# A fused attention and feed-forward kernel: another seven-product scheme in the first dense layer, chained in one PSUM bank, with a new written-out order

## The chip, the cores and the metric

One core of one Trainium2 chip. The metric is the device time of one execution in microseconds. TensorE (PE) multiplies matrices; VectorE (DVE), ScalarE (ACT) and GpSimd (POOL) work on tiles; SyncE (SP) and the POOL queue issue most transfers. Each engine works through its own instructions in the order in which the program gives them. The operands of the matrix products are bf16, the sums in PSUM fp32.

## The reference

```python
# q, k, v: (4, 8, 768, 64); n_sink 4, window 128; w_in: 512 x 2048; w_out: 2048 x 512
scores = q @ k^T / sqrt(64)                            # per batch and head, 768 x 768
keep = (key < 4) | ((query - key >= 0) & (query - key < 128))
a = softmax(where(keep, scores, -1e9))
x = (a @ v).transpose(0, 2, 1, 3).reshape(3072, 512)   # heads side by side
g = maximum(x @ w_in, 0) ** 2                          # 3072 x 2048
out = g @ w_out                                        # 3072 x 512
```

## The kernel before, in words

*How the program is put together.* The kernel first records some 945 operations (each a small function that emits one or a few instructions) and then emits them in the sequence of a written-out list of numbers, `ORDER` (L21 to L58). The suffix of a number names the engine where there is a choice (d is DVE, a is ACT, g is POOL), `+0` or `+1` the PSUM pool that a tile comes from. The tile framework adds the waits on data and on rooms; the order on each engine's queue is that of the list. `DUMMIES` (L59) gives some PE operations filler matmuls ahead of their own. Rooms are counted in L146: two PSUM tiles of two banks each in the pool att and two in den, which scores, values, products and outputs share, and in SBUF among others expm=8, qs=6, r=3.

*Batch by batch.* There are four batches of 768 rows, handled in steps of 256 rows (s = 0, 1, 2). For the attention of a step the score matmuls (L613) write PSUM, ACT takes the exponential into an `expm` room (L634), POOL (L218) or DVE masks it, the value matmuls (L682) follow, DVE normalizes (L698/L699) and the rows are turned into `xT`. Batch 0 at the very start has the longest way: q and k are loaded by SP in fp32 (qr, L351), cast to bf16 (L192, L194 or L195, the three engines' branches of one copy helper) and turned by PE (L507) for each of four pairs of heads, then copied out of PSUM. At the start POOL also makes the identity and the masks, the head rows (`build_head_rows`) and the scaled sink values (L554), and issues the loads of v, w_in and w_out. Batches 2 and 3 load q and k as rows and are turned by transposing transfers on SP (L461), and their attention outputs too (L713). The order spreads the attention of batch b+1 between the dense products of batch b.

*First dense layer.* Batch 0 has the plain form, `layer1` (L752, matmuls L763). Batches 1 to 3 have `layer1_fast` (L821), a seven-product (Strassen) form. The weights are cut into A00, A01, A10, A11 (first index: half of the 2048 features, second: half of the 512 inputs), the transposed rows into B00 to B11 (second index: half of the rows), and with sums of blocks made beforehand

```
m1 = (A00+A11)(B00+B11)   m2 = (A10+A11)B00      m3 = A00(B01-B11)   m4 = A11(B10-B00)
m5 = (A00+A01)B11         m6 = (A10-A00)(B00+B01)  m7 = (A01-A11)(B10+B11)
C00 = m1+m4-m5+m7   C01 = m3+m5   C10 = m2+m4   C11 = m1-m2+m3+m6
```

Weight sums come from `weight_sums_in` (L792, ten DVE operations once), row sums from `total` inside `layer1_fast` (three single and one double operation for each group of rows). `FAST` (L1281) names the row groups: in batch 1 steps (0, 1) as 512 rows and then step 2 as 256, in batches 2 and 3 step 0 as 256 rows and then (1, 2) as 512. Each group is worked through in quads (`quad`, L867): 18 quads, 12 with 28 matmuls over 256 columns and 6 with 56 over 128. A quad has one PSUM tile of two banks, 512 fp32 columns each. m1 goes to bank 0, m2 to bank 1; ACT or DVE copies bank 0 to an SBUF tile t (k1), DVE subtracts m2 (k2) and, when m5 has replaced m1 in bank 0, m5 (k3, both L936). m4 is added onto bank 1 and m3 onto bank 0; k4 rectifies both banks in one instruction of 1024 columns (L951 on ACT), a square follows (L917 on ACT, L919 on DVE), m6 and m7 are added on, and k5 (L963, a custom DVE operation: sum, bounded below by 0) adds t to both banks; a second square follows. All products of a quad are at L894.

*Second dense layer.* `layer2` (L969) for two steps of batch 0, `layer2_chain` (L1188, matmuls L1233) for nearly all others, `layer2_fast` (L1029) for the last. Outputs are copied to `osb` rooms and stored by SP.

Of the kernel before, what the change touches and what calls it, by code (L numbers as in the profile page):

```python
# [21 lines left out]
944 0 1 2 7 8 9 10 11 12 13 14 15 16 17 18 945+0 3 5 19 20 21 6 79 22 23 24 25 55d 56d 57+0 58 59d 60a 83+0 85 103+1  # L22
105 26 27 28 62d 61d 63+1 64 67d 68d 65a 69+0 70 71d 72d 66a 84+1 73a 74a 75+1 76 78d 91+0 86 77a 93 80 113+1 87+0
92+1 89 94 95+0 97 115 88 90 96 98 114+1 99+0 101 117 100d 104+0 81+1 102d 107 82 4 29 106g 30 31 32 33 34 35 36 37 38
39 40 41 42 43 44 45 46 127 47 48 49 50 116d 118d 108d 156+0 109+1 119+1 121 111 162+0 110 120 122 112 123+1 125 124d
126d 157a 163a 158a 164a 168+1 165+0 51 52 53 54 177+0 169a 170d 208g 166a 167a 178d 171+1 179a 172a 128+1 131+0 174+0
173a 132a 129d 319 323 321 175d 324 176d 322 130a 320 159+1 133a 160a 161a 278+0 279 136+1 144+0 145+0 280 281 148 138
146 289+1 149d 139d 274 147d 275 282 290 283 291 292 284 276 277 134+1 137+0 135 286a 140 141d 285 287d 293 150+0 151
294 142+1 196+0 192+1 295 143 193 200+1 198a 202a 195d 197 199d 201 203d 297d 194d 296 298a 152+1 154 204+0 205
212+0+1 153a 155d 189+0 215 206a 213 190a 214 207d 186+0 216 191d 248+0 187d 249d 251+1 209 253a 188d 252a 180+1 181d  # L30
250d 182d 183+0 326 184a 185d 300 301 230+0+1 233 299 288 219+0+1 231 220 304+0 210+0 306a 211 222 305 237+0+0 240
232d 325 302 221 303 223 241d 238 239d 311 307 217+1 254+0 224+0 308a 255 309 218 242+0 225 243 452g 422 423 424 425
426 427 428 429 430 431 432 433 434 234g 235+1 226+0 228 310a 227a 229a 314 236 244+0 246 316a 247a 327 313 245d 329
256+0+1 257 315 328 332 317 330 347+1 333+1 348 334 259 335a 337 312 336 331 338 349a 263+1+1 266 264 339 351 340 341a
350 352 435 436 437 258g 438 439 267g 265g 361+0 353 362 354 363d 260g 364 343 365 366 445 440 453 444 441 355a 356a
342a 448 446 449 442 447 443 451 450 318 344 345 357 375+0 358 376 261+0 359 377a 346a 367 368 379 378 262 380 268+0
270+0 381 382 360a 369a 271a 269 370d 371 272 273d 372 383a 389 373 463+0+0 385 386 466 464 390 408+0 409 394+1 395
410a 391 393 387 411 396a 397 412 456+1+0 413 392 414 398 400 415 374d 388a 457 384a 399 504 458 506 465 467 505 508+0
416a 401 418 419 510a 511 402a 654 655 684g 656 657 658 659 660 661 662 663 664 665 672 459 420 460 685 512a 417a 421a
403a 404 468+0 509 405 513 454+1 469 406 507 514a 455 515 461+0 472+1+0 407a 517 523 542 462 518 519 521 544 675 673  # L40
470 473 546+0 475 543 548a 479+0+0 516 520d 549 480 482 550a 524 481d 545 476d 525 483d 547 495+1+0 551 553 496 552a
498 556 674 676 666 667 668 474g 669 670 499g 471 522 679 488+0+0 555 554 526 497d 484+1 557 491 489 671 492g 490g
477+0 500+0 485 478 559 501 561 527+0 528 529d 563 562 493+0 565 558d 494 534 530 535 531d 566+0 567 532 533a 568d 569
564 570 572 571 536 683 682 677 678 486 502 680 711+0+0 487 503 573 574d 537 538 539d 540 681 541 560 714 712 704+0+0
580+0 581 576 577 582d 583 594 584 585 575a 705 707 688+0+0 713g 715g 706g 708g 689 691 578 586 587 626+1 627 588a
628a 612+0 686+0 613 687 630 596 692 690 595 629 631 716+0 717 589a 614a 632 633 579a 634a 635a 615 590 616 597 617
693+0 694 591 618 636 619 637 592 598+1 599 620a 600a 638 593a 601 622 640+0 641 602 623 642a 736 643 603 644 604 646
605 645 709+0 647 624 740+0 639a 621a 606a 648a 742a 649a 607a 608 609 738 737 650 651 743 739 710 610 611d 741
695+0+0 744a 625a 696 698 652 653d 755 697 699 756 757 745 747 746a 749 748 720+0+0 723 759+0 750 700+0 701 761a 762
751 721 752a 763a 760 722g 753 724g 727+0+1 774 775 758 728 730 725+0 766 764 778+1 779 765a 729d 767 776 726 777 768  # L50
731g 732+1 733 718 719 702 703 754 734 735 793 794 785 770 769 798+1 812+0 799 813 780a 771a 800a 814a 781 782a 797
796 786 772 795 815 801 802 816 817 818 803 783 819 784d 787 820a 804 805 789 822 823 829 826 827 828 791 806a 807a
821a 808 809 788 830+0 831 790a 832a 824 825d 810 858+1 811a 834 872+0 844+1 860a 846a 874a 833 835 836 837 873 845
859 876 838a 839a 886 887 888 875 877 861 840 841 848 862 864 792 773 842 863 847 889 849 878 879 890+0 865 843a 880a
850 882 883 851 892a 881a 866d 867d 884 893 894d 868 869 852a 853a 854 855 870 856 895 891 897 896a 885a 900 857d 871d
905 909+1 899 907 901 924 926 906 898 925 903 911a 912 913a 902a 928+1 904 914 910 929 931+1 915d 908 927 918 920 919
930a 933a 916 922 921d 934 917 923 932 935 936 939 937 938 943 940 942 941
"""  # L58
DUMMIES = {  # L59
    945: 29, 58: 8, 63: 10, 64: 4, 83: 3, 91: 3, 97: 3,  # L60
# [56 lines left out]
def kernel(  # L117
# [674 lines left out]
    def weight_sums_in(key, last):  # L792
# [4 lines left out]
        def room(e):  # L797
            if not tiles:
# [4 lines left out]
        spec = ((1, A[0][0], A[1][1], ALU.add, (0, 0), (0, 1)), (6, A[1][0], A[0][0], ALU.subtract, (0, 2), (1, 0)),  # L803
                (7, A[0][1], A[1][1], ALU.subtract, (1, 1), (1, 2)))
        for n, (name, x, y, how, *places) in enumerate(spec):
            for a, (d, j) in enumerate(places):
                def run(e, name=name, x=x, y=y, how=how, a=a, d=d, j=j):
                    room(e)
                    wi_sb[name, a] = tiles[d][:, j]
                    nc.vector.tensor_tensor(out=tiles[d][:, j], in0=x[:, :, a], in1=y[:, :, a], op=how)  # L810
                ops["wi", name, a] = op(key + 0.004 * (2 * n + a), {"dve": 0.7}, run, after=[w_in_op[i] for i in range(4)],
                                        takes=slots if n + a == 0 else [],
                                        follow=[ops["wi", 1, 0]] if n + a else [])
        for name, x, y, old in ((2, A[1][0], A[1][1], 6), (5, A[0][1], A[0][0], 7)):
            for a in range(2):
                def run(e, name=name, x=x, y=y, a=a):
                    wi_sb[name, a] = x[:, :, a]
                    nc.vector.tensor_tensor(out=x[:, :, a], in0=x[:, :, a], in1=y[:, :, a], op=ALU.add)
                ops["wi", name, a] = op(key + 0.03 + 0.004 * a, {"dve": 0.7}, run, after=[ops["wi", old, a]] + last)

    def layer1_fast(b, ss, key, step):  # L821
# [13 lines left out]
        whole = Slot("expm", 3 + 2 * nq)  # L835
# [9 lines left out]
        def total(names, x, y, how, n):  # L845
            pool = "qs" if len(names) * hw <= 256 else "expm"
            slot = Slot(pool, nq * len(names))
            P.group = ("xs", b, ss[0])

            def run(e):  # L850
                t = bank(slot, "xs", [128, 2 * len(names), hw], BF16)
                (nc.vector if e == "dve" else nc.gpsimd).tensor_tensor(out=t, in0=x(), in1=y(), op=how)  # L852
                for i, name in enumerate(names):
                    xs[name] = t[:, 2 * i:2 * i + 2]
            o = op(key(0) - 0.002 * (5 - n), {"dve": 0.18 + 0.26 * len(names) * hw / 256}, run,
                   after=landed, takes=[slot], reads=[whole] if len(ss) == 1 else [])
            for name in names:
                sums[name], slots[name] = o, slot
# [8 lines left out]
    def quad(b, ss, qd, key, xs, sums, slots, part, landed, whole):  # L867
# [4 lines left out]
        bs, ts, r1s, r2s = Slot(("den", "att"), 1), Slot("expm", 3), Slot("r", 1), Slot("r", 1)  # L872
# [3 lines left out]
        def weights(name, f, a):  # L876
            if name == 3:
                return w_in_sb[:, f // 4, a, f % 4:512:4]
            if name == 4:
                return w_in_sb[:, 2 + f // 4, 2 + a, f % 4:512:4]  # L880
            return wi_sb[name, a][:, f // 4, f % 4:512:4]
# [519 lines left out]
```

## Time and profile before

| what | value |
|---|---|
| time, median of 3 runs | 209.46 us (209.41 to 210.68) |
| span of the profiled execution | 208.3 us |
| granted clock of TensorE | 1.000 |
| busy: PE / DVE / ACT / POOL | 200.5 / 173.1 / 135.9 / 96.4 us |
| matmuls / DVE / ACT / POOL instructions | 2476 / 318 / 189 / 138 |
| moved by DMA | 26.10 MB |

The span goes from the first to the last instruction of one profiled execution; the time of a run holds some more, before and after. The page gives busy time by engine, the span in forty slices with the busy tenths of each, the chain of work that ended last (followed back from the end), and groups of instructions by source line. A row of a group reads: line, engine, operation, output and input with partitions x elements and type, count, then busy us and mean ns of one, then the idle time of that engine just before these instructions and what ended it. A busy PE is not PE at its peak, and the ends of matmuls are modelled.

### The profile page before, as it was taken

How to read it: one execution, taken by the hardware profiler on the slowest of the kernel's cores; microseconds unless marked ns; L12 is line 12 of the kernel's file. 1: busy time of each engine (PE TensorE's matmuls, PEld its weight loads, DVE VectorE, ACT ScalarE, POOL GpSimd, SP SyncE). 2: the span in 40 equal slices, each digit the busy share in tenths (PEclk: the TensorE clock that was granted, in tenths of full speed). 3: DMA queues.
4: the chain of work that ended last, by engine and by line, in shares of the span. 5: the costliest groups of instructions: out<-in, count | busy, mean ns of one | idle time of the engine just before them, and what ended most of it. 6: DMA issues, size and time to landing. Idle time of an engine off the chain costs nothing.

```text
span 208.3 us, 5924 instructions
## 1 busy us (share of the span) xinstructions
PE 200.5 (96%) x2476; PEld 174.3 (84%) x2476; DVE 173.1 (83%) x318; ACT 135.9 (65%) x189; POOL 96.4 (46%) x138
## 2 busy tenths in 40 slices
PE   7989999999998999999999998999999999999993
PEld 7658997457986889989878987999888999998893
DVE  6759268867599998999999987999989598999933
ACT  2695888433749589999987047988856248693110
POOL 7999274599599976689356209000043000000000
PEclk9999999999999999999999999999999999999999
DMA  6999999999999999999999945300204203200115
GB/s 190 260 184 207 173 196 215 166 146 142 261 68 148 131 172 137 181 162 121 154 116 220 109 96 134 148 3 0 50 14 145 50 5 113 88 3 0 50 54 201
DMA packets 93994, 26.10 MB, mean 125 GB/s; under 512 B 86800, under 2 KB 91408, under 8 KB 93968
## 3 DMA queue, kind: packets, MB, share of 16 engines
q0 software_dynamic: 69248, 12.59, 80.2%
q1 hardware_dynamic: 24536, 13.01, 27.9%
q8 instruction: 19, 0.31, 0.6%
q10 hardware_dynamic: 184, 0.14, 0.2%
q14 instruction: 7, 0.06, 0.1%
HBM read 27.30 MB, written 6.29 MB: 161 GB/s over the span
## 4 chain that ended last, share of the span: by engine, by line
PE 82%; DVE 5%; DMA 4%; SPq 3%; ACT 2%; issue 2%; DVEq 0%; ACTq 0%
PE py L1233 26%; PE pm L894 23%; PE pm L763 10%; PE py L984 7%; PE po L682 6%; PE ps L613 4%; DMA qr<-in_q_dram 3%; PE pt L507 2%; PE py L1094 2%; SPq L351 2%; DVE t L936 1%; PE px L731 1%; DMA xT<-xn_sb 1%; SPq L461 1%; ACT expm L634 1%
## 5 line engine op out<-in xcount | busy, mean ns | idle before, releaser
L634 ACT ACTIVATE expm<-ps 128x1024 bf16<-128x1024 f32 (+1 forms) x48 | 43.7, 953 | 7.7 <-PE ps L613 7.5
L218 POOL TENSOR_SCALAR_AFFINE_SELECT expm<-expm 128x512 bf16<-128x512 bf16 x34 | 22.7, 705 | 44.2 <-ACT expm L634 40.4
L894 PEld LDWEIGHTS <-w_in_sb 128*128 128x128 bf16 x384 | 32.2, 114 | 2.0 <-issue 1.9
L1233 PEld LDWEIGHTS <-gT_sb 128*128 128x128 bf16 x288 | 27.2, 98 | 4.7 <-issue 1.4
L917 ACT ACTIVATE gT_sb<-r 128x1024 bf16<-128x1024 bf16 x28 | 28.8, 1054 | 2.5 <-DVE r L963 2.3
L894 PE MATMUL pm<-xs,wi 128*128 128x256 bf16 (+1 forms) x288 | 29.2, 246 | 0.1
L192 ACT ACTIVATE osb<-py 128x256 f32<-128x256 f32 (+1 forms) x30 | 11.9, 399 | 25.0 <-PE py L1233 19.8
L936 DVE TENSOR_TENSOR t<-t,pm 128x512 f32<-128x512 f32 x36 | 23.8, 683 | 3.7 <-PE pm L894 2.9
L894 PEld LDWEIGHTS <-wi 128*128 128x128 bf16 x288 | 24.6, 114 | 1.0 <-DVE xs L852 0.4
L1233 PEld LDWEIGHTS <-sg 128*128 128x128 bf16 x216 | 20.3, 98 | 2.7 <-issue 0.5
L963 DVE CUSTOM_DVE_ANT_1 r<-pm,t 128x1024 bf16<-128x1024 f32 x18 | 21.8, 1218 | 0.5 <-PE pm L894 0.5
L763 PE MATMUL pm<-xT,w_in_sb 128*128 128x256 bf16 x192 | 22.0, 273 | 0.0
L763 PEld LDWEIGHTS <-w_in_sb 128*128 128x128 bf16 x192 | 20.6, 114 | 0.3 <-issue 0.2
L894 PE MATMUL pm<-xs,w_in_sb 128*128 128x256 bf16 (+1 forms) x192 | 19.9, 246 | 1.0 <-DVE t L936 1.0
L951 ACT ACTIVATE r<-pm 128x1024 bf16<-128x1024 f32 x16 | 16.3, 1022 | 4.9 <-DVE osb L194 2.3
L1233 PE MATMUL py<-w_out_sb,gT_sb 128*128 128x256 bf16 x144 | 18.7, 273 | 0.6 <-ACT expm L634 0.6
L1233 PE MATMUL py<-wt,sg 128*128 128x256 bf16 x144 | 18.7, 273 | 0.0
L1233 PE MATMUL py<-wt,gT_sb 128*128 128x256 bf16 x144 | 18.5, 273 | 0.0
L682 PEld LDWEIGHTS <-expm 128*128 128x128 bf16 x352 | 16.6, 97 | 1.9 <-issue 0.6
L682 PE MATMUL po<-v,expm 128*128 128x65 bf16 x352 | 17.8, 193 | 0.3 <-ACT expm L634 0.3
L699 DVE TENSOR_TENSOR xn_sb<-po,rc 128x512 bf16<-128x512 f32 (+1 forms) x28 | 17.2, 615 | 1.0
L984 PE MATMUL py<-w_out_sb,gT_sb 128*128 128x512 bf16 x64 | 14.8, 379 | 0.0
(104 smaller groups left out, 376.9 us busy)
## 6 DMA issues: line engine op xcount, KB each, us to landing
out_dram<-osb SPq DMA_DIRECT2D x11, 512.0 KB, 3.7
v<-in_v_dram POOLq DMA_DIRECT2D x24, 128.0 KB, 6.2
qn<-in_k_dram POOLq DMA_DIRECT2D x20, 128.0 KB, 6.1
qn<-in_q_dram POOLq DMA_DIRECT2D x20, 128.0 KB, 6.5
w_in_sb<-in_moe_w_in_dram POOLq DMA_DIRECT2D x4, 512.0 KB, 9.4
w_out_sb<-in_moe_w_out_dram POOLq DMA_DIRECT2D x4, 512.0 KB, 10.8
qr<-in_k_dram SPq DMA_DIRECT2D x4, 256.0 KB, 5.1
qr<-in_q_dram SPq DMA_DIRECT2D x4, 256.0 KB, 4.8
```

The costliest lines, as they stand in the source:

```text
L218: nc.gpsimd.affine_select(out=e_tile, in_=e_tile, compare_op=ALU.is_ge, fill=fill, base=i - 1, pattern=[[0, n], [1 if i else -1, 128]], ch ...
L634: nc.scalar.activation(out=x[:, :, o:512], in_=bank_t["s", b, s, m][:, :, o:512], func=AF.Exp, scale=scale)
L682: touch(("po", b, s, m0), e, nc.tensor.matmul(pv[:, i, h2, :], lhsT=lhsT, rhs=rhs, start=(n_ == 0), stop=(n_ == len(mms) - 1)), j)
L699: touch(("po", b, s, m0), e, nc.vector.tensor_tensor(out=xn_sb[:, 2 * s:2 * s + 2, 128 * (m0 + j0):128 * (m0 + j0 + nj)].rearrange("p i (j ...
L763: nc.tensor.matmul(pm[:, i, :], lhsT=w_in_sb[:, fb // 4, kb, fb % 4:512:4], rhs=xT[:, c0 // 256:(c0 + cw) // 256, kb, :], start=(kb == 0), ...
L894: touch(tag, e, nc.tensor.matmul(y[:, bk, i, :], lhsT=weights(name, f0 + i, a), rhs=rhs[:, a, :], start=fresh and i == 0 and a == 0, stop= ...
L917: nc.scalar.activation(out=d, in_=x, func=AF.Square)
L936: touch(tag, e, nc.vector.tensor_tensor(out=T["t"], in0=T["t"], in1=T["y"][:, bk], op=ALU.subtract), bk)
L951: touch(tag, e, nc.scalar.activation(out=r, in_=T["y"], func=AF.Relu), 0, 1)
L963: touch(tag, e, nc.vector._custom_dve(TENSOR_ADD_SAT, out=r.rearrange("p b n c -> p b (n c)"), in0=T["y"].rearrange("p b n c -> p b (n c)" ...
L984: touch((b, u), e, nc.tensor.matmul(pm[:, i, :], lhsT=gT_sb[:, fb, 128 * t:128 * t + 128], rhs=w_out_sb[:, fb, :], start=(fb == 0), stop=( ...
L1233: touch((b, u), e, nc.tensor.matmul(region(name), lhsT=x[:, i, :], rhs=w_[:, i, :], start=first and i == 0, stop=i == HB - 1, skip_group_c ...
```

## The change

The quads go over to another seven-product scheme (Winograd's form), with these blocks:

```
m1 = A00 B00   m2 = A01 B10   m4 = A11 X4   m5 = W1 X1   m6 = W2 X2   m7 = W3 X3   m3 = W4 B11
W1 = A10+A11   W2 = W1-A00    W3 = A00-A10  W4 = A01-W2
X1 = B01-B00   X2 = B11-X1    X3 = B11-B01  X4 = B10-X2
C00 = m1+m2    C01 = m1+m6+m5+m3    C10 = m1+m6+m7+m4    C11 = m1+m6+m5+m7
```

The weight sums are eight DVE operations instead of ten (six in tiles of their own, two in place). The row sums are four single operations on DVE, of which the second waits for the first and the fourth for the second.

In a quad, bank 0 is a chain: m1, copy c1, m6 added on, copy c2, m5 added on, copy c3, m3 added on, and then a rectifier over 512 columns that gives C01. Bank 1 takes m2, from which with c1 a bounded sum over 512 columns gives C00; then m7, which replaces it, and with c3 gives C11; then m4 is added on, and with c2 gives C10. So three copies a quad (ACT or DVE) where there was one, three bounded half sums on DVE where there were two subtractions and one whole bounded sum, and a half rectifier where there was a whole one. The first square now takes C00 and C11, the second C01 and C10. Products, in the order written: m1, m2, m6, m7, m5, m3, m4. All 18 quads keep their 28 or 56 matmuls. The copies take `expm` rooms, one each.

`ORDER` is new from end to end (979 operations) and with it the choice of engines: of the 54 copies c1 to c3, 45 are on ACT and 9 on DVE; of the 36 squares 18 on ACT and 18 on DVE (28 and 8 before); of the 18 half rectifiers 15 on ACT and 3 on DVE. In all DVE gets 328 instructions instead of 318 and ACT 219 instead of 190. The beginning of both lists, of which the order at the start can be read (0 to 6 constants, head rows at 6; 7 and 16 to 18 loads of sinks; 8 to 15 loads of k and q in turn; 19 on POOL's loads; 55 to 78 six for each pair of heads: cast of k, of q, two turns, two copies; 79 scaled sink values on POOL; 83 on scores, exponentials and masks):

```diff
-944 0 1 2 7 8 9 10 11 12 13 14 15 16 17 18 945+0 3 5 19 20 21 6 79 22 23 24 25 55d 56d 57+0 58 59d 60a 83+0 85 103+1
-105 26 27 28 62d 61d 63+1 64 67d 68d 65a 69+0 70 71d 72d 66a 84+1 73a 74a 75+1 76 78d 91+0 86 77a 93 80 113+1 87+0
+7 0 978 3 8 9 10 11 12 979+1 13 56a 5 1 55d 57+1 61d 67d 63+0 58 60 14 62a 15 6 65 64 66 79 19 73d 20 21 22 59a 103+1
+68 4 69+1 104+0 70 74d 105 107 83+0 75+1 71a 77 72a 113+0 76 78 108d 85 91+0 115 92+1 116d 84+1 23 80 87+0 24 93 94
```

(A number without a letter goes to the first engine that its operation allows: 68 is now a cast on POOL, where it was on DVE; 79 is on POOL in both. The sink values of one later batch go from POOL to DVE.) Further on, the four xT turns of a batch's last two steps and its q and k turns stand in another sequence on SP, and the score groups of the next batch at other places between the products.

The core of the rest of the diff:

```diff
-        spec = ((1, A[0][0], A[1][1], ALU.add, (0, 0), (0, 1)), (6, A[1][0], A[0][0], ALU.subtract, (0, 2), (1, 0)),
-                (7, A[0][1], A[1][1], ALU.subtract, (1, 1), (1, 2)))
+        spec = ((1, A[1][0], A[1][1], ALU.add, (0, 0), (0, 1)), (2, 1, A[0][0], ALU.subtract, (0, 2), (1, 0)),
+                (4, A[0][1], 2, ALU.subtract, (1, 1), (1, 2)))
...
-        total((1,), lambda: part(0, 0), lambda: part(1, 1), ALU.add, 0)
-        total((4,), lambda: part(1, 0), lambda: part(0, 0), ALU.subtract, 1)
-        total((3,), lambda: part(0, 1), lambda: part(1, 1), ALU.subtract, 2)
-        whole.readers += len(ss) == 1
-        total((6, 7), lambda: halves[0], lambda: halves[1], ALU.add, 3)
+        o1 = total(1, lambda: part(0, 1), lambda: part(0, 0), 0, [])
+        o2 = total(2, lambda: part(1, 1), lambda: xs[1], 1, [o1])
+        total(3, lambda: part(1, 1), lambda: part(0, 1), 2, [])
+        total(4, lambda: part(1, 0), lambda: xs[2], 3, [o2])
...
-        bs, ts, r1s, r2s = Slot(("den", "att"), 1), Slot("expm", 3), Slot("r", 1), Slot("r", 1)
+        bs, r1s, r2s = Slot(("den", "att"), 2), Slot("r", 1), Slot("r", 1)
...
+        def kept(name, n, after):
+            slot = cs[name] = Slot("expm", 1)
+
+            def run(e):
+                T[name] = bank(slot, "t", [128, nb, hw], FP32)
+                touch(tag, e, copy(e, T[name], T["y"][:, 0]), 0, alone=True)
+            P.group = ("t", b, ss[0])
+            return op(key(n), {"act": 0.6, "dve": 0.69}, run, after=after, takes=[slot])
+
+        def rooms_of(r, slot):
+            if r not in T:
+                T[r] = bank(slot, "r", [128, 2, nb, hw], BF16)
+            return T[r]
+
+        def bounded(r, slot, half, name, n, after, takes, reads=()):
+            def run(e):
+                d = rooms_of(r, slot)[:, half]
+                touch(tag, e, nc.vector._custom_dve(
+                    TENSOR_ADD_SAT, out=d.rearrange("p n c -> p (n c)"),
+                    in0=T["y"][:, 1].rearrange("p n c -> p (n c)"),
+                    in1=T[name].rearrange("p n c -> p (n c)"), s0=3.4028235e38, s1=0.0), 1)
+            P.group = ("t", b, ss[0])
+            return op(key(n), {"dve": 0.69}, run, after=after, takes=takes, reads=[cs[name]] + list(reads))
+
         m1 = product(1, 0, 0, True, [])
         m2 = product(2, 1, 1, True, [])
-        k1 = op(key(1), {"act": 0.6, "dve": 0.64}, first, after=[m1], takes=[ts])
-        k2 = op(key(2), {"dve": 0.7}, less(1), after=[m2, k1], reads=[ts])
-        m5 = product(5, 0, 2, True, [k1])
-        k3 = op(key(3), {"dve": 0.7}, less(0), after=[m5, k2], reads=[ts])
-        m4 = product(4, 1, 3, False, [k2])
-        m3 = product(3, 0, 4, False, [k3])
-        k4 = op(key(5), {"act": 1.04, "dve": 1.25}, relu, after=[m3, m4], takes=[r1s])
-        square(6, "r1", f0, 1, r1s, [k4])
-        m6 = product(6, 0, 6, False, [k4])
-        m7 = product(7, 1, 7, False, [k4])
-        k5 = op(key(8), {"dve": 1.25}, final, after=[m6, m7, k3], takes=[r2s], reads=[bs, ts])
-        square(9, "r2", f0 + 8, 1, r2s, [k5])
+        k1 = kept("c1", 1, [m1])
+        e1 = bounded("r1", r1s, 0, "c1", 2, [m2, k1], [r1s])
+        m6 = product(6, 0, 2, False, [k1])
+        m7 = product(7, 1, 3, True, [e1])
+        k2 = kept("c2", 3, [m6])
+        m5 = product(5, 0, 4, False, [k2])
+        k3 = kept("c3", 5, [m5])
+        e4 = bounded("r1", r1s, 1, "c3", 6, [m7, k3], [])
+        square(7, "r1", f0, 0, r1s, [e1, e4])
+        m3 = product(3, 0, 6, False, [k3])
+        m4 = product(4, 1, 7, False, [e4])
+        k4 = op(key(7), {"act": 0.6, "dve": 0.69}, relu, after=[m3], takes=[r2s], reads=[bs])
+        e3 = bounded("r2", r2s, 1, "c2", 8, [m4, k2], [], [bs])
+        e3.after.append(k4)
+        square(9, "r2", f0, 1, r2s, [k4, e3])
```

More of the change, by code (lines that the diff above doesn't have):

```diff
@@ L27 @@
[L27 to L31, printed above, removed]
@@ L809, in run @@
                     wi_sb[name, a] = tiles[d][:, j]
-                    nc.vector.tensor_tensor(out=tiles[d][:, j], in0=x[:, :, a], in1=y[:, :, a], op=how)
-                ops["wi", name, a] = op(key + 0.004 * (2 * n + a), {"dve": 0.7}, run, after=[w_in_op[i] for i in range(4)],
+                    nc.vector.tensor_tensor(out=tiles[d][:, j], in0=wi_sb[x, a] if isinstance(x, int) else x[:, :, a],
+                                            in1=wi_sb[y, a] if isinstance(y, int) else y[:, :, a], op=how)
+                ops["wi", name, a] = op(key + 0.004 * (2 * n + a), {"dve": 0.7}, run,
+                                        after=[w_in_op[i] for i in range(4)] +
+                                        [ops["wi", z, a] for z in (x, y) if isinstance(z, int)],
                                         takes=slots if n + a == 0 else [],
                                         follow=[ops["wi", 1, 0]] if n + a else [])
[L814 to L819, printed above, removed]
+        for a in range(2):
+            def run(e, x=A[1][0], y=A[0][0], a=a):
+                wi_sb[3, a] = x[:, :, a]
+                nc.vector.tensor_tensor(out=x[:, :, a], in0=y[:, :, a], in1=x[:, :, a], op=ALU.subtract)
+            ops["wi", 3, a] = op(key + 0.03 + 0.004 * a, {"dve": 0.7}, run, after=[ops["wi", 1, a]] + last)
     def layer1_fast(b, ss, key, step):
@@ L834, in spread @@
             halves.extend((t[:, :, 0], t[:, :, 1]))
-        whole = Slot("expm", 3 + 2 * nq)
+        whole = Slot("expm", 4 + 3 * nq)
         P.group = ("xs", b, ss[0])
@@ L843, in part, with total @@
             return halves[j][:, 2 * i:2 * i + 2]
[L845 to L847 removed]
+        def total(name, x, y, n, after):
+            slot = Slot("qs", nq + {1: 1, 2: 1}.get(name, 0))
             P.group = ("xs", b, ss[0])
             def run(e):
[L851 to L858, printed above, removed]
[L859 to L863 removed]
+                t = bank(slot, "xs", [128, 2, hw], BF16)
+                nc.vector.tensor_tensor(out=t, in0=x(), in1=y(), op=ALU.subtract)
+                xs[name] = t
+            o = op(key(0) - 0.002 * (5 - n), {"dve": 0.18 + 0.26 * hw / 256}, run, after=landed + after, takes=[slot],
+                   reads=([whole] if len(ss) == 1 else []) + [slots[z] for z in (1, 2) if name == {1: 2, 2: 4}[z]])
+            sums[name], slots[name] = o, slot
+            return o
+        o1 = total(1, lambda: part(0, 1), lambda: part(0, 0), 0, [])
+        o2 = total(2, lambda: part(1, 1), lambda: xs[1], 1, [o1])
+        total(3, lambda: part(1, 1), lambda: part(0, 1), 2, [])
+        total(4, lambda: part(1, 0), lambda: xs[2], 3, [o2])
         for qd in range(nq):
@@ L890, in run @@
                 y = T["y"]
-                rhs = xs[name] if not direct else part(0, 0) if name == 2 else part(1, 1)
+                rhs = xs[x] if x else part(*{1: (0, 0), 2: (1, 0), 3: (1, 1)}[name])
                 for i in range(nb):
@@ L897, in run @@
                             skip_group_check=not (fresh and i == 0)), bk)
-            need = [w_in_op[0], w_in_op[1], w_in_op[2], w_in_op[3]] if name in (3, 4) else [ops["wi", name, a] for a in range(2)]
-            o = op(key(n), {"pe": 0.45}, run, after=after + need + (landed if direct else [sums[name]]) + last[-1:],
-                   takes=[bs] if name == 1 else [],
-                   reads=[slots[name]] if not direct else [whole] if len(ss) == 1 else [])
+            wi = {5: 1, 6: 2, 7: 3, 3: 4}.get(name)
+            need = [ops["wi", wi, a] for a in range(2)] if wi else [w_in_op[i] for i in range(4)]
+            o = op(key(n), {"pe": 0.45}, run, after=after + need + ([sums[x]] if x else landed) + last[-1:],
+                   takes=[bs] if name == 1 else [], reads=[slots[x]] if x else [whole] if len(ss) == 1 else [])
             last.append(o)
@@ L925, in quad @@
         m1 = product(1, 0, 0, True, [])
         m2 = product(2, 1, 1, True, [])
-        P.group = ("t", b, ss[0])
-        def first(e):
-            T["t"] = bank(ts, "t", [128, nb, hw], FP32)
-            touch(tag, e, copy(e, T["t"], T["y"][:, 0]), 0)
-        k1 = op(key(1), {"act": 0.6, "dve": 0.64}, first, after=[m1], takes=[ts])
-        def less(bk):
-            def run(e):
-                touch(tag, e, nc.vector.tensor_tensor(
-                    out=T["t"], in0=T["t"], in1=T["y"][:, bk],
-                    op=ALU.subtract), bk)
-            return run
```

90 lines of the change are left out of this document (43 added, 47 removed).

## The prediction

> **What bounds the kernel now.** First the page: span, busy shares, the forty slices, the chain.
>
> ```profile
> span 208.3 us, 5924 instructions
> PE 200.5 (96%) x2476; PEld 174.3 (84%) x2476; DVE 173.1 (83%) x318; ACT 135.9 (65%) x189; POOL 96.4 (46%) x138
> ...
> PE   7989999999998999999999998999999999999993
> ...
> DVE  6759268867599998999999987999989598999933
> ACT  2695888433749589999987047988856248693110
> ...
> PEclk9999999999999999999999999999999999999999
> ...
> PE 82%; DVE 5%; DMA 4%; SPq 3%; ACT 2%; issue 2%; DVEq 0%; ACTq 0%
> ```
>
> The span is 208.3 us and the median time 209.46, so some 1.2 us lie outside the span; I make the sum against the span and add it to the median. TensorE (PE) is the bound: full clock, 82% of the chain. VectorE (DVE) and ScalarE (ACT) run close behind it in the slices from about 73 us on, but being busy is not yet being late. How late they are is told by the busy times in stretches (columns: stretch, length, PE, PEld, DVE, ACT, POOL):
>
> ```profile
> 16.60:60.00 43.40, 43.40 (x465) 34.67 (x462) 29.80 (x51) 25.97 (x35) 29.59 (x41) 1.00 1.72 177
> 60.00:64.00 4.00, 3.03 (x42) 2.26 (x39) 3.88 (x7) 2.97 (x4) 4.00 (x6) 1.00 2.03 129
> 64.00:89.00 25.00, 24.99 (x351) 22.46 (x351) 23.77 (x45) 21.31 (x32) 19.60 (x27) 1.00 1.86 158
> 89.00:91.00 2.00, 1.85 (x25) 1.59 (x24) 2.00 (x5) 2.00 (x4) 1.67 (x2) 1.00 1.49 184
> 91.00:128.00 37.00, 37.00 (x555) 32.48 (x554) 33.97 (x65) 26.81 (x37) 20.86 (x29) 1.00 1.58 130
> 128.00:132.00 4.00, 3.03 (x40) 2.39 (x36) 3.73 (x6) 3.00 (x4) 1.71 (x3) 1.00 0.83 292
> 132.00:203.20 71.20, 71.20 (x826) 66.25 (x823) 62.85 (x108) 43.05 (x62) 4.08 (x6) 1.00 0.14 43
> ```
>
> From 16.6 us, where the dense work starts, to 203.2 PE stands still only 0.97+0.15+0.97+0.01 = 2.1 us. That is nearly all that a new order inside this stretch can win. The matmul ends in this view are modelled, so the loss is a little more. The critical chain in order of time shows both large holes:
>
> ```profile
> 61.03 0.74 ACT r L775
> ...
> 61.95 1.03 ACT expm L634
> ...
> 63.02 1.03 PE py L1233 x8
> ...
> 125.65 2.50 DMA xT<-xn_sb
> ...
> 129.14 0.69 DVE t L936
> 129.87 1.92 PE pm L894 x20
> ```
>
> The first is a rectifier and an exp on ACT that free PSUM; the second a subtraction of the quad chain (L936), late because DVE stood behind a transfer that landed at 128.15. From 60.92 to 63.02 PE issues 20 small score matmuls that elsewhere take about 0.85 us, from 128.26 to 129.87 eight that take 0.45: losses of 1.25 and 1.15. With 0.3 at 89 us that makes 2.7 us removable (bounds: 2.1 by the table, 3.1 if every late issue counts).
>
> **The change part by part.** *PE work.* Seven products a quad stay seven; 18 quads, 12 with 28 and 6 with 56 matmuls, are 672 as before, and all 2476 and the 60 fillers stay. Price 0.
>
> *DVE and ACT work in the quads.* The rows that price it:
>
> ```profile
> L936 DVE TENSOR_TENSOR t<-t,pm 128x512 f32<-128x512 f32 x36 | 23.8, 683 | 3.7 <-PE pm L894 2.9
> L963 DVE CUSTOM_DVE_ANT_1 r<-pm,t 128x1024 bf16<-128x1024 f32 x18 | 21.8, 1218 | 0.5 <-PE pm L894 0.5
> L951 ACT ACTIVATE r<-pm 128x1024 bf16<-128x1024 f32 x16 | 16.3, 1022 | 4.9 <-DVE osb L194 2.3 <-PE pm L894 1.9 <-DVE r L953 0.4
> L192 ACT ACTIVATE t<-pm 128x512 f32<-128x512 f32 x15 | 8.5, 597 | 0.2
> L194 DVE COPY t<-pm 128x512 f32<-128x512 f32 x3 | 2.1, 689 | 0.7 <-PE pm L894 0.7
> L917 ACT ACTIVATE gT_sb<-r 128x1024 bf16<-128x1024 bf16 x28 | 28.8, 1054 | 2.5 <-DVE r L963 2.3
> L919 DVE TENSOR_TENSOR gT_sb<-r 128x1024 bf16<-128x1024 bf16 x8 | 5.6, 714 | 0.2
> ```
>
> Removed: 36 subtractions and 18 whole bounded sums. Added: 54 half bounded sums, all on DVE; 54 copies instead of 18 (45 on ACT, 9 on DVE); 18 half rectifiers (15 on ACT). The squares move from 28 ACT and 8 DVE to 18 and 18. A half sum is in no row: it is no less than half of 1.218 = 0.61 and no more than the 0.69 of the 512-wide copy; I take 0.685, by the equally wide L936. DVE: before 36x0.683 + 18x1.218 + 2x1.22 + 3x0.69 + 8x0.714 = 56.7, after 54x0.685 + 9x0.69 + 3x0.69 + 18x0.714 = 58.2 us. ACT: before 15x0.597 + 16x1.022 + 28x1.054 = 54.9, after 45x0.597 + 15x0.60 + 18x1.054 = 54.9. So the quads give neither engine relief; work that the new order moves from DVE to ACT elsewhere (unloads, output copies) makes it about -2 us on DVE and +4 on ACT in all. Price 0, covered by PE: DVE has 208.3-173.1 = 35 us and ACT 72 us of idle time. If that cover fails it is the second rival.
>
> The fixed part of each instruction speaks against splitting: L963 is 1.218 for 1024 and the 512-wide rows are 0.68 to 0.69, more than half. [...]
>
> *Weight and input sums.* 10 weight sums become 8 and the doubled input sum becomes singles, one waiting on another: about -3 us of DVE in stretches where PE does not wait. Price 0.
>
> *The startup.* Here the new order costs time. Rows of the view in order of time:
>
> ```profile
> 5.05 0.68 DVE L194 COPY qkT<-pt 128x512 bf16<-128x512 bf16 x1
> 7.02 2.20 DVE L194 CAST qs<-qr 128x512 bf16<-128x512 f32 x4 [1.28 <-DMA qr<-in_q_dram]
> 7.37 1.72 ACT L634 ACTIVATE expm<-ps 128x768 bf16<-128x768 f32 x2 [0.48 <-PE ps L613]
> 17.37 0.38 ACT L580 ACTIVATE es<-pk 128x256 bf16<-128x256 f32 x1
> 2.53 0.61 POOL L254 COPY sg<-sg 128x512 bf16<-128x512 bf16 x1
> 6.91 2.02 POOL L554 TENSOR_TENSOR vs<-vs_in,head_rows 32x130 bf16<-32x130 f32 x4
> 16.16 1.70 POOL L218 TENSOR_SCALAR_AFFINE_SELECT expm<-expm 128x512 bf16<-128x512 bf16 x2
> 42.83 1.43 POOL L259 COPY mask<-tri 128x256 bf16<-128x256 bf16 x1
> ```
> ```profile
> 16.62 1.87 PE pm L763 x16
> 18.50 1.45 PE po L682 x48
> 19.95 1.75 PE pm L763 x16
> ```
>
> Before, DVE casts the first k and q and copies that pair's transposes at 5.05, and ACT begins its exps at 7.37, packed from there to 17.75. In the new order DVE casts three k loads before that first copy. The third k is issued at 2.95, and its cast was at 8.05 behind others; by the 4.7 us that the q load before it took, I put its landing at 7.7. Then cast 0.55 and copy 0.68: 8.9, and the 0.48 that lay between copy and exp before: first exp at 9.35. ACT then has the old 10.38 us less one unload (0.6) and two casts (1.28), 8.5 in all, plus 0.3 for the second exp, which waits for two more DVE copies: the sink exp ends at 18.15, the last big exp at 17.8. All four value groups of the second 256 rows now stand *before* the first dense matmul, and the third needs a POOL mask on that last exp (1.70: 19.5); it and the fourth, 0.36 each, end at 20.2. Before, everything but the first 16 dense matmuls was done at 19.95, so like for like 19.95-1.75 = 18.2. Startup: +2.0 us. Bounds: +0.8 (third k 0.8 earlier, since POOL's v loads no longer compete, and no further wait) and +3.7. The upper end comes from POOL: it now does head rows and L554 before its loads, reaching the new cast (L195) at about 10.3; that cast is in no row, between the 0.61 of L254 and twice L259 = 2.9. I take 0.61, the same size, and it is then just hidden; at 2.9 ACT waits 1.7 longer. [...]
>
> The weight loads behind that on POOL leave 2 to 4 us later; they are wanted 2.0 later as well and DMA empties the same backlog, so 0, or up to +1 if not.
>
> *The middle.* In the built program at least as many other products stand between a product and the one that waits for its copy as the 0.6 copy and hand-over need, and the places of 63, 89 and 129 us are ordered anew, the four xT transposes together on SP ahead of the last qkT ones: -2.7. On the other side four waits a quad make 72 places, some short by 0.1 to 0.3 us, banks handed over with no slack about as often as before, and one more switch into score matmuls (0.2): I take +1.0 (bounds 0.2 and 3).
>
> *Tail.* Last products, sums and stores are as before: 0.
>
> Sum: +2.0 - 2.7 + 1.0 = +0.3 on the span, 208.6; on the median 209.46+0.3, **209.8 us**.
>
> **The rivals.** *Faster:* startup at its low end, old holes closed, no new ones: +0.8-2.7+0.2 = -1.7, 207.8. For it speaks that POOL's loads leave DMA to q and k at first; against it the in-order DVE, which waits for the third k in any case. 0.15.
> *Slower, the quads become bound by ACT and DVE:* from 64 to 89 us they were busy 21.31 and 23.77 of 25 already. A quad gets 0.27 us more of both together (4.2 before, without squares, 4.45 after) and its path crosses from PE to ACT or DVE and back at every product. If the copies queue behind squares, so that one product in each quad waits 0.15 us more than I allowed, the 18 quads lose 2.7 us, and the sum is +2.0-2.7+1.0+2.7 = +3.0: 212.4. It decides from a mean loss of 0.1 us a quad (1.8 us) beyond my 1.0. 0.22.
> *Startup at its upper end* (L195 slow): +3.7-2.7+1.0 = +2.0, 211.5. 0.08.
> *The change does nothing that counts* is inside the likeliest: DVE is not relieved in the quads, and it was not the bound.
>
> **How the numbers follow.** Likeliest, startup loss and closed holes nearly cancelling: 0.55, own range 208.0 to 211.4. About 1% (2.1 us) is what I take a measurement of this kernel to tell. Faster by more (under 207.4): half of the first rival and a remnant, 0.09. Slower by more (over 211.55): nearly all of the second rival, half of the third, 0.06 of the likeliest: 0.30. Within: 0.61. The range 207.7 to 212.5 leaves out 2 in 10.
>
> **What would show it.** First exp near 9.3 and first dense matmul near 20 us; PE idle under 1.5 us between there and the last product; half sums near 0.685; ACT and DVE totals near 140 and 171. I am wrong if the dense work starts before 18.8, or if PE waits on ACT copies or half sums by more than 2 us in all.

## The result and the profile after

The changed kernel takes 218.05 us (median of 4 runs, 217.63 to 219.02), the kernel before 209.78 beside it: ratio 1.038, 95% interval 1.0335 to 1.0426. That is 8 us slower, where I had forecast 209.8 and a range up to 212.5. The ratios and their intervals, here and below, leave out the few executions over 1.5% above their kernel's fastest, which the medians include. The profiled execution has a span of 216.1 us against 208.3. First its page:

```profile
span 216.1 us, 5944 instructions
PE 203.7 (94%) x2471; PEld 173.9 (80%) x2476; DVE 171.9 (80%) x328; ACT 138.2 (64%) x218; POOL 95.5 (44%) x131
...
PE   7689999999999999899999999998999999999993
...
DVE  3567747779589878889899897978799988787673
ACT  3396369357998569796995268787972236787100
...
PE 65%; ACT 13%; DVE 12%; issue 4%; DMA 2%; SPq 1%; ACTq 0%; DVEq 0%
```

DVE and ACT have about as much to do as before: DVE has 171.9 us of work (173.1), ACT 138.2 (135.9). PE has the same matmuls, though their records add up to 203.7 us instead of 200.5. In the chain that ended last PE has 65% instead of 82%, and ACT and DVE together 25% instead of 7%. The busy times in stretches (columns as before) tell where:

```profile
20.30:79.00 58.70, 58.42 (x651) 47.00 (x654) 45.42 (x78) 39.72 (x59) 43.10 (x55) 1.00 1.60 148
79.00:104.00 25.00, 22.99 (x299) 20.23 (x297) 20.99 (x41) 20.04 (x34) 17.91 (x24) 1.00 1.86 153
104.00:133.00 29.00, 28.86 (x426) 24.66 (x424) 25.73 (x53) 20.01 (x30) 12.11 (x17) 1.00 1.51 139
133.00:152.00 19.00, 17.52 (x218) 15.65 (x217) 16.71 (x32) 14.91 (x25) 2.16 (x3) 1.00 0.46 87
152.00:200.00 48.00, 47.41 (x537) 43.22 (x536) 42.22 (x78) 29.45 (x50) 3.72 (x4) 1.00 0.16 48
```

PE loses 2.0 us between 79 and 104 us and 1.5 between 133 and 152, where the half sums stand closest: 15 and 13 of the 54, one in 1.5 to 1.7 us. In these two stretches DVE and ACT stand still more than PE does: 4.0 and 5.0 us in the first, 2.3 and 4.1 in the second. Three engines that stand still in one place may be waiting for each other in turn. The view shows less than is lost. The record of four of the quads' matmuls lasts 0.60 us, but the next four begin 0.43 to 0.44 us after them (the PE rows below), so each stop of PE hides about 0.16 us (an estimate, 0.60-0.44); which may be why PE's busy time is larger.

One hole shows the circle. Rows of DVE, ACT and PE in order of time (start, length, what; in brackets the idle time before and its releaser):

```profile
141.13 1.29 DVE L941 CUSTOM_DVE_ANT_0 r<-pm,t 128x512 bf16<-128x512 f32 x2 [0.62 <-ACT r L966]
146.44 0.69 DVE L941 CUSTOM_DVE_ANT_0 r<-pm,t 128x512 bf16<-128x512 f32 x1 [1.39 <-ACT t L192]
```
```profile
140.51 0.59 ACT L966 ACTIVATE r<-pm 128x512 bf16<-128x512 f32 x1
141.86 1.06 ACT L914 ACTIVATE gT_sb<-r 128x1024 bf16<-128x1024 bf16 x1 [0.76 <-DVE r L941]
142.95 0.60 ACT L966 ACTIVATE r<-pm 128x512 bf16<-128x512 f32 x1
143.44 0.59 ACT L192 ACTIVATE t<-pm 128x512 f32<-128x512 f32 x1
143.92 2.01 ACT L914 ACTIVATE gT_sb<-r 128x1024 bf16<-128x1024 bf16 x2
145.82 0.59 ACT L192 ACTIVATE t<-pm 128x512 f32<-128x512 f32 x1
```
```profile
145.11 0.60 PE L891 MATMUL pm<-xT,w_in_sb 128*128 128x256 bf16 x4
145.54 0.60 PE L891 MATMUL pm<-xs,w_in_sb 128*128 128x256 bf16 x4
147.19 0.60 PE L891 MATMUL pm<-xs,w_in_sb 128*128 128x256 bf16 x4 [1.04 <-DVE r L941]
```

Read it from the top. DVE's half sum waits 0.62 us for ACT's half rectifier (L966, from 140.51). ACT's square then waits 0.76 for that half sum. From there ACT is late, does two more squares (2.01), and only then the copy of 145.82, for which DVE's next half sum waits 1.39, and PE for that half sum. The first of these waits is the odd one. The rectifier reads bank 0 of the quad's PSUM tile and writes one half of r; the half sum reads bank 1 and writes the other. Neither has anything of the other's. The waits of the whole execution (engine's line, whom it waited for, us in total, times, longest), first DVE, then ACT:

```profile
DVE r L941 <- ACT t L192: 6.0, 7, 1.4
DVE r L941 <- ACT r L966: 5.4, 8, 1.1
```
```profile
ACT t L192 <- DVE r L941: 2.8, 4, 1.6
ACT r L966 <- DVE r L941: 1.7, 1, 1.7
```

A half sum needs the copy that it adds (first row). The other three rows, 9.9 us of DVE and ACT idle, show no data in common: copies and rectifier use bank 0 alone, half sums read bank 1. (A copy may also wait for a room that an older half sum gives back; 0.4 us, as will be seen.) They come from the program. In this kernel instructions of two engines on one PSUM tile are ordered unless they are declared independent: of the 2.8 us that copies wait for half sums, 0.4 is left once the pairs are declared (cross waits taken away, below). The helper `touch` declares pairs off PE only where both carry `alone=True`; in the diff the copies and the rectifier carry it, and the half sums in `bounded` do not. In the kernel before, this could not show: its subtractions and its sum over both banks stood in one chain of data with the copy and the rectifier anyway.

So two theories stood. **W**: these cross waits between DVE and ACT cost most of the 8 us. **Q**, my second rival: copies stand behind squares and exponentials in ACT's in-order queue, and the waits only show who came last.

### The profile page after: what moved, and what is told of

Same layout as the page of the kernel before. It is cut to its first block, busy times and chain, and to the rows that moved or that the text cites. A ratio compares the mean times of both kernels' runs of the same rounds, so it can differ in the third digit from the quotient of the medians.

```text
span 216.1 us, 5944 instructions
## 1 busy us (share of the span) xinstructions
PE 203.7 (94%) x2471; PEld 173.9 (80%) x2476; DVE 171.9 (80%) x328; ACT 138.2 (64%) x218; POOL 95.5 (44%) x131
## 4 chain that ended last, share of the span: by engine, by line
PE 65%; ACT 13%; DVE 12%; issue 4%; DMA 2%; SPq 1%; ACTq 0%; DVEq 0%
PE py L1238 20%; PE pm L891 14%; PE pm L763 10%; PE py L989 6%; PE po L682 5%; DVE r L941 4%; PE ps L613 4%; ACT t L192 4%; ACT gT_sb L914 3%; ACT expm L634 3%; DMA qr<-in_k_dram 2%; ACT r L966 2%; PE py L1099 2%; PE pt L507 2%; PE px L731 1%
## 5 line engine op out<-in xcount | busy, mean ns | idle before, releaser
L941 DVE CUSTOM_DVE_ANT_0 r<-pm,t 128x512 bf16<-128x512 f32 x54 | 36.1, 686 | 13.3 <-ACT t L192 6.0
L218 POOL TENSOR_SCALAR_AFFINE_SELECT expm<-expm 128x512 bf16<-128x512 bf16 x30 | 22.0, 763 | 53.5 <-ACT expm L634 50.6
L192 ACT ACTIVATE t<-pm 128x512 f32<-128x512 f32 x45 | 26.0, 601 | 15.2 <-PE pm L891 9.1
L192 ACT ACTIVATE osb<-py 128x256 f32<-128x256 f32 (+1 forms) x35 | 13.8, 403 | 19.2 <-PE py L1238 15.2
L891 PE MATMUL pm<-xs,w_in_sb 128*128 128x256 bf16 (+1 forms) x192 | 21.2, 246 | 2.1 <-DVE r L941 2.0
L1238 PEld LDWEIGHTS <-sg 128*128 128x128 bf16 x216 | 20.2, 98 | 3.2 <-issue 0.6
L891 PE MATMUL pm<-xs,wi 128*128 128x256 bf16 (+1 forms) x192 | 20.9, 246 | 0.0
L914 ACT ACTIVATE gT_sb<-r 128x1024 bf16<-128x1024 bf16 x18 | 18.7, 1059 | 1.3 <-DVE r L941 1.3
L1238 PE MATMUL py<-wt,gT_sb 128*128 128x256 bf16 x144 | 18.7, 273 | 0.6 <-DVE osb L1252 0.4
L1238 PE MATMUL py<-wt,sg 128*128 128x256 bf16 x144 | 18.7, 273 | 0.2 <-ACT osb L192 0.2
L613 PE MATMUL ps<-qkT 64*128 64x128 bf16 (+1 forms) x256 | 14.8, 238 | 2.1 <-DVE qkT L194 1.3
L613 PEld LDWEIGHTS <-qkT 64*128 64x128 bf16 x256 | 8.3, 94 | 8.6 <-issue 6.6
```

Of the source, the lines that this page charges most:

```text
L192: return nc.scalar.activation(out=dst, in_=src, func=AF.Copy)
L218: nc.gpsimd.affine_select(out=e_tile, in_=e_tile, compare_op=ALU.is_ge, fill=fill, base=i - 1, pattern=[[0, n], [1 if i else -1, 128]], ch ...
L613: nc.tensor.matmul(ps[:, h2, o:o + w], lhsT=qkT_sb[r, m, 1, c, :], rhs=qkT_sb[r, m, 0, qb:qb + w // 128, :], start=(i == 0 and not biased) ...
L891: touch(tag, e, nc.tensor.matmul(y[:, bk, i, :], lhsT=weights(name, f0 + i, a), rhs=rhs[:, a, :], start=fresh and i == 0 and a == 0, stop= ...
L914: nc.scalar.activation(out=d, in_=x, func=AF.Square)
L941: touch(tag, e, nc.vector._custom_dve(TENSOR_ADD_SAT, out=d.rearrange("p n c -> p (n c)"), in0=T["y"][:, 1].rearrange("p n c -> p (n c)"), ...
```

## The experiments

All changes are to the changed kernel. They ran in three sets, in which the kernel before took 210.35, 210.41 and 210.50 us. A difference between two of them is the difference of their ratios to the kernel before, times 210.4 us; the measure is the changed kernel run again. It ran in the second set alone, so the cross waits taken away, the two kinds apart and the old start by itself, which ran in the first, are compared with it across two sets.

**The changed kernel again.** 

> The changed kernel unchanged, as the measure for the others on this chip. All theories: 3.3 to 4.3% over the kernel before, a span near 216.

Measured: 217.87 us, ratio 1.0344 (1.0311 to 1.0377).

**Cross waits taken away.**

```diff
-                touch(tag, e, copy(e, T[name], T["y"][:, 0]), 0, alone=True)
+                touch(tag, e, copy(e, T[name], T["y"][:, 0]), 0, alone=True, part=name)
...
-                    in1=T[name].rearrange("p n c -> p (n c)"), s0=3.4028235e38, s1=0.0), 1)
+                    in1=T[name].rearrange("p n c -> p (n c)"), s0=3.4028235e38, s1=0.0), 1, alone=True, part=name)
```

> The changed kernel with one difference: the half sums on DVE (bank 1 of a quad's PSUM tile) are declared independent of the copies and the half rectifier (bank 0) that have no data in common with them. Only the half sum that reads a copy still waits for that copy. Theory W (the two engines wait for each other over banks that they do not share): the 25 or so waits of half sum on rectifier, rectifier on half sum and second copy on first half sum go, and the kernel gains 4 to 6.5 us, to about 211.5 to 214. Theory Q (copies stand behind squares and exponentials in ACT's in-order queue, my second rival): these waits only show who came last, the queue is as full as before, and the gain is under 1.5 us (216.5 or more). Holes of PE near 81, 86, 89, 146 us: gone by W, still there by Q.

Measured: 212.0 us, ratio 1.0053 (1.0008 to 1.0099); (1.0344-1.0053)x210.4 = 6.1 us less than the changed kernel, and 7.3 by the spans of the profiled executions (216.1 and 208.8, the shortest of its ten, which reach 213.6). The 6.1 is W's number, far from Q's. The two stretches that correspond, and DVE's waits:

```profile
79.00:104.00 25.00, 24.79 (x351) 22.88 (x348) 23.28 (x45) 22.76 (x38) 17.55 (x24) 1.00 1.86 150
...
130.00:150.00 20.00, 19.84 (x252) 18.36 (x251) 19.71 (x38) 18.05 (x29) 1.83 (x3) 1.00 0.49 92
```
```profile
DVE r L941 <- ACT t L192: 3.0, 4, 1.2
DVE r L941 <- PE pm L891: 1.7, 5, 0.5
DVE r L941 <- ACT gT_sb L914: 0.8, 2, 0.4
```

PE's idle time there is 0.2 and 0.2 us. The row of the rectifier is gone (the rows before have 13 cross waits with idle time, not the 25 or so expected), and even the true wait for the copy is halved: the copies had been late because they had themselves waited for half sums. With the copies alone freed, in the next pair of runs, it is halved too (2.9). On ACT one wait of a copy for a half sum is left, a room:

```profile
ACT t L192 <- DVE r L941: 0.4, 1, 0.4
```

**The two kinds of cross wait apart.** To free the rectifier alone, copies and half sums share one part, so that they stay ordered (the diff). To free the copies alone, the edit above is kept and the rectifier loses its `alone=True`.

```diff
+                touch(tag, e, copy(e, T[name], T["y"][:, 0]), 0, alone=True, part="half")
...
+                    in1=T[name].rearrange("p n c -> p (n c)"), s0=3.4028235e38, s1=0.0), 1, alone=True, part="half")
```

> Only the half rectifier and the half sums are declared independent; copies and half sums still wait for each other over the banks. Theory W: about half of the gain, -2 to -3.5 us (214.5 to 216), since the rectifier ahead of the last half sum of a quad is the wait that the DVE rows name 8 times (5.4 us of idle DVE), but it is partly the same lost time. Theory Q: under 1 us.

Measured: 215.8 us, ratio 1.0234 (1.016 to 1.0307). 

> The other half: copies and half sums without common data are declared independent, the rectifier still waits for the half sums and they for it. Theory W: -2 to -3.5 us (214.5 to 216), and the two halves together less than, equal to or, if each wait hides the other, more than the sum. Theory Q: under 1 us.

Measured: 216.72 us, ratio 1.0302 (1.0233 to 1.0371), short of what W expected. One kind gives 2.3 us, the other 0.9, which the intervals do not tell from nothing, and both together 6.1. That is 2.9 more than the sum, just beyond the intervals taken together (an estimate from the four of them: 2.4). It fits a circle that still closes with one kind left. The rectifier and the last half sum of a quad also write one tile r, and the edit frees them there as well; how much of their wait came from r was not tried. Copies and half sums without common data share the PSUM tile alone. DVE's longest waits in the first and in the second:

```profile
DVE r L941 <- ACT t L192: 6.6, 7, 1.4
```
```profile
DVE r L941 <- ACT r L966: 5.7, 8, 1.3
DVE r L941 <- ACT t L192: 2.9, 4, 1.2
```

**Squares on ACT made light**, with the cross waits and without them.

```diff
-                    nc.scalar.activation(out=d, in_=x, func=AF.Square)
+                    nc.scalar.activation(out=d[:, :, :, 0:hw // 4], in_=x[:, :, :, 0:hw // 4], func=AF.Square)
```

> The changed kernel with the cross waits kept; the squares on ACT write and read only a quarter of their columns (three quarters of those 18 squares are left out). Theory Q (copies queue behind squares): the squares are the 2 us pieces ahead of the late copies, so the gain is about that of taking the waits away, 4 to 6 us, to a span of 210 to 212. Theory W: the squares only stretch a chain of waits; the rectifier and half sum waits stay: 1.5 to 2.8 us, to 213.3 to 214.7.

> The same light squares on ACT, with the cross waits taken away. Theory W: without the waits ACT has slack, light squares gain under 0.5 us on the kernel with only the waits taken away (span 208.8). Theory Q: the queue is still the limit, and the squares are worth another 1.5 us or more (207.3 or less).

Both kernels leave out three quarters of these squares, and so do not compute the result; they only price ACT's time. Measured: 216.09 us with the waits, ratio 1.0242 (1.0207 to 1.0277), 2.1 us less than the changed kernel; 212.38 without them, ratio 1.0034 (0.9997 to 1.0072), 0.4 us from the full squares and within the intervals. The row of these squares in the changed kernel, and in the first of the two:

```profile
L914 ACT ACTIVATE gT_sb<-r 128x1024 bf16<-128x1024 bf16 x18 | 18.7, 1059 | 1.3 <-DVE r L941 1.3
```
```profile
L914 ACT ACTIVATE gT_sb<-r 128x256 bf16<-128x256 bf16 x18 | 7.3, 417 | 2.5 <-DVE r L941 2.4
```

18.7-7.3 = 11.4 us of work are off ACT's queue, and the time falls by 2.1 and, without the waits, by nothing that can be told. The queue behind the squares was real in the trace, but without the cross waits its length makes no difference that can be told. Q falls.

**The old start.** The first 116 entries of the old order, then the new order without them; the loads of later batches stay where the new order has them.

> The changed kernel with the order of before for the first 116 entries (batch 0 up to its first dense products; loads of later batches left where they are), waits as they are. My prediction's startup step (+2.0): the first dense matmul goes back from 20.3 to about 16.6 to 17 us with 16 products ahead of the last value groups, and the time falls by 1.4 to 2.1 us, to 216 to 216.7. Rival: what is gained there is given back at the waits of the quads further on, and the time falls by less than 0.7 us.

Measured: 216.81 us, ratio 1.0302 (1.0236 to 1.0368), 0.9 us less than the changed kernel, under the 1.4 expected; the intervals overlap, so this run alone does not settle the step. The first dense products of its profiled execution start at 18.81 us, not at the 16.6 to 17 expected, since it met late transfers. The last load of q, issued at the same time, in the chains of the kernel before and of this one:

```profile
4.48 6.15 DMA qr<-in_q_dram
```
```profile
4.48 7.65 DMA qr<-in_q_dram
```

1.5 us between two executions of the same start, as much as the step that was to be measured. So the step is better read from many executions, and with the waits away:

> Half sums declared independent of the copies and the rectifier without common data, and the first 116 entries of the order as before. Theory W with my startup step: the cross waits and the startup are all that the change loses, so both taken back leave the closed holes: 1.2 to 2.2 us under the kernel with the waits taken away alone (span 208.8), a span of 206.6 to 207.6, 0.3 to 1% faster than the kernel before. Rival: the start depends on when the first q and k transfers land, not on the order of the casts; then the span stays at 208 to 209.

Measured: 210.01 us, ratio 0.9979 (0.9946 to 1.0011): 1.6 us under the same kernel with the new start (across two sets, and the intervals overlap by a little), as expected. Against the kernel before it is 0.2% faster, which is not told from no change, so the 0.3 to 1% expected is not shown. The span of its profiled execution, 209.5 us, is one of the longer of twelve (207.4 to 210.4) and lies above the expected; of this the late loads are a part (its last q took 8.07 us), and a stop near 122 us, where scores wait for a turned q or k:

```profile
4.50 8.07 DMA qr<-in_q_dram
...
116.14 6.69 DMA qkT<-qn
122.83 0.04 issue
122.87 0.45 PE ps L613 x8
```

**What is late next.** The transfers that SP issues in the 7 or 8 us there, with their median time to landing, in the changed kernel and then in the last experiment, where they leave earlier:

```profile
out_dram<-osb SPq DMA_DIRECT2D x1, 512.0 KB, 3.5
qkT<-qn SPq DMA_TRANSPOSE x3, 4.6
```
```profile
out_dram<-osb SPq DMA_DIRECT2D x1, 512.0 KB, 5.5
...
qkT<-qn SPq DMA_TRANSPOSE x3, 8.4
```

In the changed kernel POOL has issued the last of its loads by 106.12 us, and the first of these turns of q and k is issued at 108.65, 2.5 us later. In the last experiment SP issues its turns from 105 us on, beside the v loads that POOL issues at 104 to 106, and those two loads take 8.6 us to land (median; 5.7 in the changed kernel). One more run moves two of those loads behind POOL's next mask (operations 686 and 687 behind 509 in the order):

> The kernel with the cross waits taken away and the old start, and the two v loads of batch 3 that POOL issues at 104 to 106 us moved behind its next mask, at 112.5. In the run without this the turns and the store that SP issues from 105 us take 5.5 to 9 us to land instead of 3.5 to 4.7 in the changed kernel, where they were issued later. If that backlog is what is late next, they land 1 to 2 us earlier, the hole at 122 us (0.8) closes, and the kernel is 0.3 to 0.9 us faster than the one before it (210.01), 0.4 to 0.8% faster than the kernel before the change. Rival: the next k and q loads now leave 1.8 us later and the turns that wait for them are late instead; no gain or a loss of up to 1 us.

Measured: 210.01 us, ratio 0.9966 (0.9933 to 1.0). In the profiled execution the transfers do land sooner:

```profile
out_dram<-osb SPq DMA_DIRECT2D x1, 512.0 KB, 4.2
...
qkT<-qn SPq DMA_TRANSPOSE x2, 6.6
```

In its profiled execution scores no longer wait for a turn near 122 us. But the median is the same; by the ratios it is 0.3 us less, within the intervals. It is the best version found, and not clearly faster than the kernel before.

## Why the prediction was wrong, point by point

*Work of the engines: right.* The new instruction cost what I took from the neighbouring row; the rows of the changed kernel:

```profile
L941 DVE CUSTOM_DVE_ANT_0 r<-pm,t 128x512 bf16<-128x512 f32 x54 | 36.1, 686 | 13.3 <-ACT t L192 6.0 <-ACT r L966 5.4 <-PE pm L891 1.1
...
L195 POOL CAST qs<-qr 128x512 bf16<-128x512 f32 x1 | 0.6, 607 | 0.0
```

0.686 us against 0.685, and for POOL's cast my 0.61 was right (0.607). DVE and ACT totals came to 172 and 138 us (171 and 140 forecast). And the last column of the first row, 13.3 us of idle time ahead of half sums, shows where the time went, though not all of it is lost time: 1.1 us are waits for PE.

*Startup, +2.0: right in size.* Rows of ACT, the chain and PE in the changed kernel:

```profile
9.76 1.02 ACT L634 ACTIVATE expm<-ps 128x1024 bf16<-128x1024 f32 x1 [1.40 <-PE ps L613]
...
17.88 0.41 ACT L580 ACTIVATE es<-pk 128x256 bf16<-128x256 f32 x1
```
```profile
2.95 5.27 DMA qr<-in_k_dram
...
20.31 1.75 PE pm L763 x16
```

First exp 9.76 (9.35 forecast), sink exp done at 18.29 (18.15), first full run of dense products at 20.31 (20.2), like for like 2.1 us late. The third k landed at 8.22, 0.5 later than I had put it, which is within what the landings vary by. My lower bound had it 0.8 earlier, because POOL's v loads would no longer compete; no trace shows that: POOL issued them from 6.14 us on instead of 3.45, and the eight q and k loads took 5.4 us to land (median) instead of 4.9. Putting the old start back gave 1.6 us once the cross waits were away, and 0.9 with them, which by itself is not told from nothing.

*Old holes closed, -2.7, and new waits, +1.0: about 1.3 us too hopeful without the cross waits, far off with them.* In the profiled execution without cross waits PE stands still 0.4 us between 20.3 and 200 (2.1 from 16.6 to 203.2 before), and the span of 208.8 is close to my sum of 208.6. That closeness is luck, since it is the shortest of ten executions. By the ratios the kernel without cross waits is 1.1 us over the kernel before, and with the old start back 0.4 under (from 1.1 under to 0.2 over), where the two terms promise 1.7 under. So together they promised about 1.3 us too much even there; which of the two is off stays open. **The step that failed is the +1.0 for new waits (bounds 0.2 and 3).** I counted waits of products on copies, of half sums on copies, and banks handed over; no wait between a half sum and a copy or rectifier on the other bank is in the sum. I took it, without a row that shows it, that instructions on different banks are not ordered, as the helper's other uses declare it. The change has 30 more copies on ACT between 54 half sums on DVE, and every half sum was ordered against its neighbours on ACT. Priced by the runs, the cross waits are 6.1 us by the ratios (7.3 by two single executions), none of it in my 1.0. (The 0.2 that I put in it for one more switch into score matmuls was an estimate: in the kernel before PE comes to such a group about 0.1 us late, at 60.92, 65.27 and 88.40 us, after dense matmuls at 0.109 us each.) My own sign of being wrong stood in the trace. PE was to wait for copies and half sums by no more than 2 us and to be idle under 1.5 us between about 20 us and the last product; it waited 2.4 in all, most of it in the row below, and was idle 4.5 between 20.3 and 200. It could be seen beforehand: of the three places in the new code, copy, half sum and rectifier, the half sum alone lacks the word that the two others have.

```profile
PE pm L891 <- DVE r L941: 2.0, 3, 1.0
```

*The second rival* (212.4, from 0.1 us lost a quad) named the place, copies behind squares on ACT, and some of the way, but not the cause: light squares gain nothing that can be told once the waits are gone. Its 2.7 us was also too small: I let each quad lose alone, while a late copy may delay the next quad's half sum too, which no run shows by itself.

*Engine totals as cover.* I hid 58 us of DVE and 55 of ACT work behind PE by their idle time in all. That cover is real only where an engine may run ahead, and the cross waits took that away: without them PE stands still 0.2 us in each of the two stretches, with hardly less work on DVE and ACT (171.2 and 138.0 us).

In the run with the cross waits away ACT on bank 0 and DVE on bank 1 are not ordered against each other, and the kernel gains 6.1 us. No run here leaves the two unordered on one bank.

What was not tried: the new scheme in the whole of the old order. So scheme and order are told apart only at the start.

## What to carry to other kernels

Count, for each new instruction, not only the data that it needs but every wait that the program will give it: here two engines on one PSUM tile were ordered unless something declared otherwise, even on separate banks, with 9.9 us of DVE and ACT idle. When three engines stand still in the same stretch and none has more work than before, look in the waits for a pair that shares no data, and take that wait away before moving work between them. Two such waits can each seem worth little alone (2.3 and 0.9 us here, 6.1 together).

## What the runs showed of the hardware

The last q load, issued at 4.48 to 4.50 us in the same order of work, took 6.15, 6.21, 7.65 and 8.07 us to land in four executions, so a single trace of this startup is good to no better than 1.5 to 2 us. Turning transfers of q and k took 4.6 us to land (median of three) when POOL's loads had been issued some 2.5 us before the first of them, 8.4 (of three) when SP issued its turns beside the last of these loads, and 6.6 (of two) with two of the loads moved away.
